# Which queue carries the empty instruction between two halves, and when a small transform may borrow a PSUM bank, in a combined convolution and feed-forward kernel

## The chip, the core and the metric

The kernel runs on one core of one Trainium2 chip. A core has a matrix engine (TensorE, PE in the profile), a vector engine (VectorE, DVE), an activation engine (ScalarE, ACT), a general engine (GpSimd, POOL) and a queue for transfers (SyncE, SP). Each engine takes the instructions of its own queue, and instructions on different engines are tied to each other by semaphores. Matmuls write to PSUM, a memory of banks from which VectorE and ScalarE read. The metric is the device time of one execution in microseconds; of the kernel before three executions are shown, and one more was recorded by the profiler.

## The reference

The input is a sequence of 2048 tokens of width 576. Two layers are run one after the other; each adds a long convolution block and a feed-forward block (FFN) to the stream:

```python
def _A_ref(q, k, v, shift_k, ssm_k, ssm_D):
    ...
    for t in range(ks):
        k_shift = k_shift + k_pad[:, t:t + S, :] * shift_k[:, ks - 1 - t][None, None, :]
    kv = k_shift * v
    ...
    y_f = kv_f * kf_f[None, :, :, :]
    y = (lambda x, s, axes=(-2,-1): jnp.fft.irfft2(x, s=s, axes=axes).astype(jnp.bfloat16))(y_f, (1, L), axes=(1, 2))[:, 0, :S, :]
    y = y + kv * ssm_D[None, None, :]
    return q * y

def _B_ref(x, w_gate, w_up, w_down):
    return (_gelu(x @ w_gate) * (x @ w_up)) @ w_down

x = A_q
x = x + _A_ref(_layernorm(x, axis=-1), A_k, A_v, A_shift_k, A_ssm_k, A_ssm_D)
x = x + _B_ref(_layernorm(x, axis=-1), B_w_gate, B_w_up, B_w_down)
x = x + _A_ref(_layernorm(x, axis=-1), A_k, A_v, A_shift_k, A_ssm_k, A_ssm_D)
x = x + _B_ref(_layernorm(x, axis=-1), B_w_gate, B_w_up, B_w_down)
```

The convolution's inner part (kv, its transform and the product with the transformed filter) is the same in both layers, since it doesn't depend on x. The inner width of the FFN is 4608.

## The kernel before

**Units and visits.** The tokens are cut into four chunks of 512, so that there are eight units (two layers by four chunks). The FFN of a unit is done in three phases of 1536 inner columns each, so that the weights of a phase can be shared between the units of a pass. There are five passes, with one, two, two, two and one units, and so 24 visits (here numbered from 1), each one unit by one phase. Visits 1 to 3 are the first unit's, 4 to 9 those of the next two units, 10 to 15 and 16 to 21 those of the passes after, and 22 to 24 the last unit's.

A visit has two stages. In the gate/up stage twelve tiles of 128 inner columns by 512 tokens are made, each by 18 matmuls that use 64 of PE's 128 rows at a time (L1081, tile gu). ScalarE applies the gelu and VectorE multiplies with the up half; the result, hT, stays in SBUF. There are two forms of this: in one (L1673, L1674) VectorE reads the up half out of PSUM and so is the one that frees the bank; in the other (L1664 to L1666) ScalarE copies the up half out too, and the bank is free before VectorE has come to it. The planner takes the second form where ScalarE is not booked far ahead (L1659 to L1674).

In the down stage (`two_rows`, called for rows 0 and 1 and then for rows 2 and 3) the four groups of 128 tokens are multiplied with the down weights, 192 half-row matmuls (L1735, tile dn) in all. A row group is accumulated in two steps: in step 0 the upper 64 rows of one operand half go to one bank and the lower 64 to the other, in step 1 the other way round. Between the two steps of the same bank pair stands `conv.hold`, an instruction that does nothing, on another engine's queue: it is made to name the bank pair, so that it waits for PE's step 0, and PE's step 1 waits for it. The transforms of the convolution (`both_steps`, `half_rows`; the matmul of `half_rows` is L310, tile cps) have the same two steps and the same instruction between them. In the trace it is an EVENT_SEMAPHORE of L1110. There are 150 of them: 54 of transforms and 96 of row groups.

When a row group is complete, VectorE adds it to the residual stream out of PSUM: L1771 in the first phase, L1773 or L1752 in the later ones, and L1765 in the last phase, where it also sums the row for the next layernorm.

**Layernorm statistics.** GpSimd computes the mean (`mean_after`, L911, tiles means and nm), ScalarE squares and sums (`square_task`, L919, tile junk), and GpSimd makes the reciprocal root from it (L926 tile ve, L927 tile rstd). The GpSimd instructions, with some DMAs, lie in a list (`conv.spills`) and are put into the program `AHEAD` = 2.0 us before the planner expects their input.

**Convolution among the visits.** The transforms, their products and the inverse of the convolution are cut into small pieces which the planner puts between tiles and row groups (`fill`). PE does the matmuls of a piece into a bank pair, ScalarE or VectorE takes the result out (eo L329, ab and cd L334, kc L633, and others). `fold` (L559, L560) is a group of eight additions and subtractions of VectorE, four for each of its two parts.

**PSUM.** There are four pairs of banks. Three of them rotate between the gate/up tiles and the row groups (`pr`, which sets `was[0]` to the time at which the planner expects the pair to be free). The fourth belongs to the convolution (`cps`). Where `conv.alt` is set, the next piece takes the next rotating pair in place of the fourth (`other`): here this is called borrowing. The pair after it then goes to a row group or a gate/up tile one place earlier in the rotation.

**What sets the order.** Nothing is moved by a compiler: the program is written in the order in which a planner, `Pace`, walks along. It keeps one clock each for PE, VectorE and ScalarE (`t.pe`, `t.dve`, `t.act`) and adds the constants C_... to them as it writes instructions. A piece is put in when its inputs are expected and its cost ends before a limit. `hurry()` is true until the planner has written the last row of the second chunk's convolution output. Each engine's queue is then in the order of writing. A changed clock anywhere can therefore change which piece comes next, on any engine.

Of the kernel before, what the change touches and what calls it, by code (L numbers as in the profile page):

```python
# [22 lines left out]
HW = 288  # L23
# [10 lines left out]
C_P0, C_P1, C_AC = 1.28, 1.35, 0.7  # L34
C_TT, C_ST, C_BN, C_NORM, C_HT, C_GELU, C_EVA, C_EVD, C_YH = 0.74, 0.80, 0.47, 0.62, 0.615, 0.51, 0.56, 0.72, 0.7
C_HB = 0.345
C_FOLD = 0.38
C_TURN, DRAIN = 0.0, 0.35
LAG = 0.25
AHEAD = 2.0  # L40
# [94 lines left out]
class Conv:  # L135
# [259 lines left out]
    def step(self, m, kv=None, loaded=False):  # L395
# [155 lines left out]
        def fold(sg):  # L551

            def run():
                if sg == 0:
                    w["free"] = self.acp.tile([P, 2, D], BF16, tag="ac", name="w")[:, 0, :]
                for plane in range(2):
                    a, b = z[plane, 0, sg][:], z[plane ^ sg, 1, sg][:]
                    up, down = (sg, sg + 2) if sg == 0 or plane else (sg + 2, sg)
                    nc.vector.tensor_tensor(out=w["free"], in0=a, in1=b, op=ALU.add)  # L559
                    nc.vector.tensor_tensor(out=a, in0=a, in1=b, op=ALU.subtract)  # L560
                    w[up, plane], w[down, plane], w["free"] = w["free"], a, b

                def fin(when):
                    for part in range(2):
                        mark(("z", sg, part), when + LAG)
                    if sg:
                        self.z_at[m] = when
                return fin
            return run
# [18 lines left out]
        for sg in range(2):  # L588
            self.V.append((now, 4 * C_FOLD, fold(sg)))
        ab = {}  # L590
# [175 lines left out]
def ssm_geglu_kernel(ctx, tc, A_q, A_k, A_v, A_shift_k, A_ssm_k, A_ssm_D, B_x, B_w_gate, B_w_up,  # L766
                     B_w_down, out):
    nc = tc.nc
# [21 lines left out]
    t = Pace()  # L790
# [10 lines left out]
    def bank(n, name, shape=(P, 2, 512), dt=F32):  # L801
        return banks[n].tile(list(shape), dt, tag="pr", name=name)
# [12 lines left out]
    def add_late():  # L815
        ready, n, run = late.popleft()
        run()
        bank_at[n % 3] = t.on_dve(C_EVD, ready) + 0.15

    bank_at, was = [0.0] * 3, [0.0]  # L820

    def pr(name):
        while late and taken[0] - late[0][1] >= 2:
            add_late()
        taken[0] += 1
        was[0] = bank_at[taken[0] % 3]
        bank_at[taken[0] % 3] = NEVER
        return bank(turn[(taken[0] - 1) % 3], name)
# [11 lines left out]
    conv = Conv(tc, ctx, t, gwork, xtp, A_k, A_v, A_shift_k, A_ssm_k, A_ssm_D, ident,  # L840
                lambda *form: bank(turn[3], "cps", *form), ypool)
# [265 lines left out]
        conv.ps_free[0] = xn_at[ui]  # L1107
        xn_done[ui] = j + 1

    conv.hold = lambda ps: nc.scalar.keepalive_nop([nc.scalar.lower_ap(ps[:, :, 0:HW])])  # L1110
    conv.slot = lambda: taken[0] % 3
    conv.borrowed = bank_at.__setitem__
    conv.alt_at = lambda: bank_at[(taken[0] + 1) % 3]
# [27 lines left out]
    def fill(limit, tensor, conv_first, between=None):  # L1141
        conv.run_open(t.pe)
        weights()
        conv.run_loads()
        spreads(tensor=tensor)
        while pressing() and run_aq(min(limit, t.pe + 2.3)):
            pass
        while True:
            if run_late(limit):
                continue  # L1150
            if conv_first:
                if not (conv.run_v(limit) or run_vq(limit)):
                    break
            elif not (run_vq(limit) or not pressing() and conv.run_v(limit)):
                break
        run_aq(min(limit, t.pe + 2.3))
        conv.between = between is not None
        if tensor and between is not None and not (1 in conv.z_at or conv.dry(between)):
            return
        if tensor:  # L1160
            for _ in range(3):
                if pressing() and (units[coming[0]][1], RT - 1) in conv.y_at or not conv.run_p():
                    break
# [16 lines left out]
    with tc.manual_schedule():  # L1180
# [6 lines left out]
        with ExitStack() as es:  # L1187
# [40 lines left out]
            ps = bank(3, "ps")  # L1228
# [379 lines left out]
        hurry = lambda: (1, RT - 1) not in conv.y_at  # L1608
# [4 lines left out]
        for at, (wb, ph, ui, first, final) in enumerate(visits):  # L1613
# [76 lines left out]
            def opened(j):  # L1690
                if j not in accs:
                    accs[j] = pr("dn"), taken[0]
                return accs[j]

            def row(j):

                acc, mine = opened(j)
                xh = x_c[c][:, j, :].rearrange("p (h d) -> p h d", h=2)

                def down(fi, h, acc):  # L1700
                    nc.tensor.matmul(acc[:, h, 0:HW], lhsT=hT[:, fi, j * P:(j + 1) * P],  # L1701
                                     rhs=wd[2 * wb + fi // WT][:, fi % WT, h * HW:(h + 1) * HW],
                                     start=(fi == 0), stop=(fi == FP - 1))
                if j == RT - 1:
                    dst = out2[c * CH:(c + 1) * CH, :].rearrange("(p j) d -> p j d", j=RT)[:, j, :]
                    for h in range(2):
                        if h:
                            acc = pr("dn")
                        for fi in range(FP):
                            down(fi, h, acc)  # L1710
                        ob, entry = out_tile()
                        entry[0] = True
                        nc.vector.tensor_tensor(out=ob[:, 0:HW], in0=xh[:, h, :], in1=acc[:, h, 0:HW], op=ALU.add)
                        nc.sync.dma_start(out=dst[:, h * HW:(h + 1) * HW], in_=ob[:, 0:HW])
                    return
                for fi in range(FP):
                    for h in range(2):
                        down(fi, h, acc)
                    t.pe += C_DN
                    if fi < FP - 1:  # L1720
                        fill(t.pe + 1.5, True, conv.left > 0)
                evict(j)

            def two_rows(j):

                order = ([(0, 0, fi) for fi in range(FP - 2)] + [(1, 0, fi) for fi in range(FP - 3)] +
                         [(0, 0, fi) for fi in range(FP - 2, FP)] + [(1, 0, fi) for fi in range(FP - 3, FP)] +
                         [(n, 1, fi) for n in range(2) for fi in range(FP)])
                for k, (n, step, fi) in enumerate(order):
                    acc, mine = opened(j + n)  # L1730
                    wn = wd[2 * wb + fi // WT][:, fi % WT, :]
                    lhs = hT[:, fi, (j + n) * P:(j + n + 1) * P]
                    for g in range(2):
                        r = slice((step ^ g) * HK, (step ^ g) * HK + HK)
                        nc.tensor.matmul(acc[:, g, 0:HW], lhsT=lhs[r], rhs=wn[r, g * HW:(g + 1) * HW],  # L1735
                                         start=step == 0 and fi == 0, stop=step == 1 and fi == FP - 1)
                    if step == 0 and fi == FP - 1:
                        conv.hold(acc)
                    t.pe += C_DN / 2
                    if step == 1 and fi == FP - 1:  # L1740
                        evict(j + n)
                    elif k % 2:
                        conv.alt = other
                        fill(t.pe + 1.5, True, conv.left > 0)

            def evict(j):
# [30 lines left out]

            conv.alt = other
            two_rows(0)
            if wb == NWB - 1:  # L1780
                conv.alt = None
                row(2)
                row(3)
            else:
                two_rows(2)
# [3 lines left out]
@with_exitstack  # L1789
def kernel(  # L1790
    ctx: ExitStack,
    tc: tile.TileContext,
    A_q: bass.AP,
    A_k: bass.AP,
    A_v: bass.AP,
    A_shift_k: bass.AP,
    A_ssm_k: bass.AP,
    A_ssm_D: bass.AP,
    B_x: bass.AP,
    B_w_gate: bass.AP,  # L1800
    B_w_up: bass.AP,
    B_w_down: bass.AP,
    out: bass.AP,
):
    ssm_geglu_kernel(tc, A_q, A_k, A_v, A_shift_k, A_ssm_k, A_ssm_D, B_x, B_w_gate, B_w_up,
                     B_w_down, out)
# [30 lines left out]
```

## Time and profile before

| what | us |
|---|---|
| median of the three runs | 913.64 |
| lowest and highest of them | 913.34 to 914.93 |
| profiled execution, whole | 913.37 |
| its span in the trace | 911.5 |
| one visit without gaps: gate/up stage, down stage | 23.31 + 11.76 |

A row of the timeline reads: start in us, duration in us, engine, line, operation, tile written and tiles read, shape, xN for N instructions drawn together, and in brackets how long the engine had been idle before it and which instruction's end released it. Where PE is concerned the ends are modelled, so the length of a gap is taken here from the starts of the groups and from the time that one more matmul in a group takes. An engine name with a q behind it (ACTq, POOLq) is that engine's sequencer, which runs the semaphore events. The span is split at the start of the first visit, 40.2 us after the span's start, ahead of which the first layernorm, the load of the inputs and the first convolution work lie; the last visit's work ends near 908.

### The profile page before, as it was taken

To read this page: it belongs to the slowest core of one execution; us is meant where nothing else is said; L and a number is where in the kernel's file an instruction comes from. 1 tells how busy PE (TensorE), PEld (TensorE's weight loads), DVE (VectorE), ACT (ScalarE), POOL (GpSimd) and SP (SyncE) were. 2 spreads that over 40 slices of the span, in tenths; PEclk is the share of its full clock that TensorE was granted. 3 is DMA by queue.
4 is the path that set the end of the run, shared out by engine and by line. 5 is a ranking of instruction groups with operands and counts; after the bars stand their busy time and mean duration, and the time that the engine had idled before them with its cause. 6 is when DMAs were issued, how large, how long until landed. Compare 5 with 4: busy or idle time off the path is not lost.

```text
span 911.5 us, 24246 instructions
## 1 busy us (share of the span) xinstructions
PE 904.0 (99%) x10451; PEld 600.2 (66%) x10451; DVE 565.1 (62%) x1129; ACT 363.2 (40%) x675; POOL 146.8 (16%) x311
## 2 busy tenths in 40 slices
PE   9999999999999999999999999999999999999998
PEld 7757656466576675765766757757757657667666
DVE  8888985885789886677888843553332334433332
ACT  7785445735425356354244223451121224321211
POOL 5533003220113012230023001220000002100000
PEclk9999999999999999999999999999999999999999
DMA  9999977449619604974934702772720820777630
GB/s 247 307 250 275 249 164 144 113 126 235 201 53 231 142 2 79 271 186 106 247 121 117 167 16 58 129 137 60 142 79 2 157 79 13 143 176 180 136 101 27
DMA packets 125839, 129.12 MB, mean 142 GB/s; under 512 B 40866, under 2 KB 118051, under 8 KB 125732
## 3 DMA queue, kind: packets, MB, share of 16 engines
q1 hardware_dynamic: 116706, 92.63, 47.8%
q0 software_dynamic: 8880, 34.36, 11.4%
q8 instruction: 81, 1.33, 0.6%
q10 hardware_dynamic: 146, 0.59, 0.2%
q14 instruction: 26, 0.21, 0.1%
HBM read 106.91 MB, written 11.80 MB: 130 GB/s over the span
## 4 chain that ended last, share of the span: by engine, by line
PE 94%; DVE 4%; ACT 1%; issue 1%; POOL 0%; ACTq 0%
PE gu L1081 58%; PE dn L1735 29%; PE cps L310 2%; PE ps L284 2%; DVE kvt L255 1%; PE dn L1701 1%; DVE kvt L261 1%; DVE kc L633 0%; PE ps L1317 0%; DVE hT L1666 0%; DVE cd L334 0%; PE ps L1452 0%; PE ps L1081 0%; DVE hh L633 0%; POOL rstd L1537 0%
## 5 line engine op out<-in xcount | busy, mean ns | idle before, releaser
L1081 PE MATMUL gu<-xnT,wgu 64*128 64x512 bf16 x5148 | 561.0, 376 | 1.1 <-DVE hT L1674 0.9
L1081 PEld LDWEIGHTS <-wgu 64*128 64x128 bf16 x5220 | 293.5, 94 | 262.3 <-issue 2.3
L1735 PE MATMUL dn<-wd,hT 64*128 64x288 bf16 x4512 | 294.6, 283 | 0.8 <-ACTq L1110 0.4
L1735 PEld LDWEIGHTS <-hT 64*128 64x128 bf16 x4512 | 253.3, 94 | 28.7 <-issue 1.6
L1673 ACT ACTIVATE ga<-gu 128x512 f32<-128x512 f32 x175 | 104.4, 597 | 318.9 <-PE gu L1081 312.7
L1674 DVE TENSOR_TENSOR hT<-ga,gu 128x512 bf16<-128x512 f32 x175 | 120.0, 686 | 172.5 <-ACT ga L1673 172.0
L1664 ACT ACTIVATE ga<-gu 128x512 bf16<-128x512 f32 x111 | 66.2, 597 | 148.4 <-PE gu L1081 140.6
L1666 DVE TENSOR_TENSOR hT<-ga 128x512 bf16<-128x512 bf16 x112 | 46.9, 421 | 54.7 <-ACT ga L1665 54.7
L1665 ACT CAST ga<-gu 128x512 bf16<-128x512 f32 x111 | 64.4, 580 | 0.0
L911 POOL TENSOR_SCALAR means<-s 128x1 f32<-128x1 f32 x28 | 16.9, 606 | 245.1 <-DVE x_c L1765 216.8
L1773 DVE TENSOR_TENSOR x_c<-x_c,dn 128x576 f32<-128x576 f32 x32 | 23.9, 751 | 26.3 <-PE dn L1735 26.2
L1771 DVE SCALAR_TENSOR_TENSOR x_c<-dn,means,x_c 128x576 f32<-128x576 f32 x28 | 22.8, 815 | 24.5 <-PE dn L1735 24.4
L927 POOL TENSOR_TENSOR rstd<-ve,neghalf_t 128x1 f32<-128x1 f32 x56 | 34.9, 623 | 4.7
L329 ACT ACTIVATE eo<-cps 128x576 f32<-128x576 f32 x40 | 25.6, 657 | 21.3 <-PE cps L310 16.7
L346 DVE TENSOR_TENSOR prod<-prod 128x576 bf16<-128x576 bf16 x64 | 29.3, 458 | 2.2
L1752 DVE TENSOR_TENSOR xn<-x_c,dn 128x576 bf16<-128x576 f32 x15 | 11.3, 753 | 26.0 <-PE dn L1735 23.6
L633 DVE TENSOR_TENSOR kc<-ab,cd 128x288 bf16<-128x288 f32 x64 | 25.5, 451 | 0.0
L444 POOL DMA_DIRECT2D kr<-Kd x20 | 11.0, 552 | 85.9 <-DVE prod L345 85.9
L911 POOL TENSOR_SCALAR nm<-s 128x1 f32<-128x1 f32 x28 | 7.9, 281 | 94.8 <-DVE x_c L965 94.7
L919 ACT ACTIVATE junk<-x_c,nm 128x576 bf16<-128x576 f32 x28 | 21.5, 767 | 4.0 <-POOL nm L911 3.5
L955 ACT ACTIVATE yh<-y,rstd 128x576 f32<-128x576 bf16 x28 | 21.2, 768 | 2.3 <-PE dn L1735 1.4
L449 POOL DMA_DIRECT2D hr<-Hd x32 | 17.6, 551 | 21.4 <-DVE prod L345 19.9
(180 smaller groups left out, 629.9 us busy)
## 6 DMA issues: line engine op xcount, KB each, us to landing
wgu<-in_B_w_gate_dram SPq DMA_DIRECT2D x45, 576.0 KB, 6.0
wd<-in_B_w_down_dram SPq DMA_DIRECT2D x30, 864.0 KB, 6.5
wgu<-in_B_w_up_dram SPq DMA_DIRECT2D x45, 512.0 KB, 9.0
hr<-Hd POOLq DMA_DIRECT2D x32, 288.0 KB, 4.7
kr<-Kd POOLq DMA_DIRECT2D x24, 288.0 KB, 4.5
Kd<-kc POOLq DMA_DIRECT2D x12, 288.0 KB, 5.1
k<-in_A_k_dram POOLq DMA_DIRECT2D x3, 1008.0 KB, 10.9
wgu<-in_B_w_up_dram SPq DMA_DIRECT2D x45, 64.0 KB, 7.9
```

Of the source, the lines that this page charges most:

```text
L329: nc.scalar.activation(out=eo[:], in_=ps[:, :, 0:HW], func=ACT.Copy, scale=scale)
L346: nc.vector.tensor_tensor(out=dst[:, cols], in0=pr[:, 0, cols], in1=pr[:, 1, cols], op=ALU.subtract if part == 0 else ALU.add)
L633: nc.vector.tensor_tensor(out=into[k][:, plane, cols], in0=a, in1=b, op=op)
L911: nc.gpsimd.tensor_scalar(out=v["nm"][:], in0=v["s"][:], scalar1=-1.0 / D, scalar2=None, op0=ALU.mult)
L927: nc.gpsimd.tensor_tensor(out=v["rstd"][:], in0=ve[:], in1=neghalf_t[:, 0:1], op=ALU.pow)
L1081: nc.tensor.matmul(cols(pair[:, s, :]), lhsT=w[r0:r0 + HK, k, gi * P:(gi + 1) * P], rhs=cols(xnT[r0:r0 + HK, blk_of[k], :]), start=(k == 0 ...
L1664: nc.scalar.activation(out=ga[:, 0, :], in_=pair[:, 0, :], func=ACT.Gelu_apprx_tanh)
L1665: nc.scalar.copy(out=ga[:, 1, :], in_=pair[:, 1, :])
L1666: nc.vector.tensor_tensor(out=hT[:, fi, :], in0=ga[:, 0, :], in1=ga[:, 1, :], op=ALU.mult)
L1673: nc.scalar.activation(out=ga[:], in_=pair[:, 0, :], func=ACT.Gelu_apprx_tanh)
L1674: nc.vector.tensor_tensor(out=hT[:, fi, :], in0=ga[:], in1=pair[:, 1, :], op=ALU.mult)
L1735: nc.tensor.matmul(acc[:, g, 0:HW], lhsT=lhs[r], rhs=wn[r, g * HW:(g + 1) * HW], start=step == 0 and fi == 0, stop=step == 1 and fi == FP - 1)
```

## The change

Four edits. The empty instruction goes to ScalarE's queue only where the planner's clock for ScalarE is not over 0.1 us ahead of that of PE, and to GpSimd's queue otherwise. In the down stage a transform may borrow a rotating pair only in the second pair of rows, or where `hurry()` is true; before, it might in both. When a row group is opened, PE's clock is set to the time at which its bank pair is expected to be free, if that is later; before, only gate/up tiles did this. The cost that the planner books for one of the fold's operations is 0.46 and not 0.38.

```diff
-C_FOLD = 0.38
+C_FOLD = 0.46
...
-    conv.hold = lambda ps: nc.scalar.keepalive_nop([nc.scalar.lower_ap(ps[:, :, 0:HW])])
+    def hold(ps):
+
+        eng = nc.scalar if t.act <= t.pe + 0.1 else nc.gpsimd
+        eng.keepalive_nop([eng.lower_ap(ps[:, :, 0:HW])])
+    conv.hold = hold
...
             def opened(j):
                 if j not in accs:
                     accs[j] = pr("dn"), taken[0]
+                    t.pe = max(t.pe, was[0])
                 return accs[j]
...
                     elif k % 2:
-                        conv.alt = other
+                        conv.alt = other if hurry() or j == 2 else None
                         fill(t.pe + 1.5, True, conv.left > 0)
```

The changed program has as many instructions on PE as before (20904 rows of its queue), and 93 of the empty instructions on ScalarE's queue and 57 on GpSimd's.

## The prediction

> **What bounds the kernel now.** I read the page's engine table and its chain of waits first, then the list of what the matmul engine waited for, then the timeline around each of those waits.
>
> ```profile
> span 911.5 us, 24246 instructions
> PE 904.0 (99%) x10451; PEld 600.2 (66%) x10451; DVE 565.1 (62%) x1129; ACT 363.2 (40%) x675; POOL 146.8 (16%) x311
> PEclk9999999999999999999999999999999999999999
> PE 94%; DVE 4%; ACT 1%; issue 1%; POOL 0%; ACTq 0%
> ```
>
> PE is busy for 904.0 of 911.5 us, it is 94% of the chain that ended last, and its clock is never cut. The change leaves PE's work as it is, so only the gaps in PE's order can shrink or grow.
>
> ```profile
> PE gu L1081 <- DVE hT L1674: 0.9, 1, 0.9
> PE dn L1735 <- ACTq L1110: 0.4, 1, 0.4
> PE cps L310 <- ACTq L1110: 0.4, 1, 0.4
> PE dn L1735 <- DVE x_c L1771: 0.3, 2, 0.2
> ```
>
> (columns: total us, times, longest). These four, behind a start-up wait and a wait at the end that the change does not touch, are all that the profile calls waits of PE after its loops begin. Two are the empty instruction (L1110) on ScalarE's queue, one is the fold, two times it is a row's eviction: the change aims at each. What one of them really costs is read from the next rows, since a matmul row's end is modelled.
>
> ```profile
> 65.69 0.42 PE L1735 MATMUL dn<-wd,hT 64*128 64x288 bf16 x4
> 66.49 0.30 PE L310 MATMUL cps<-ht,T 64*128 64x288 bf16 x2 [0.38 <-ACTq L1110]
> 338.72 1.89 PE L1735 MATMUL dn<-wd,hT 64*128 64x288 bf16 x28
> 183.77 0.53 PE L1735 MATMUL dn<-wd,hT 64*128 64x288 bf16 x6
> 184.71 1.40 PE L1735 MATMUL dn<-wd,hT 64*128 64x288 bf16 x20 [0.42 <-ACTq L1110]
> ```
>
> A group of 28 takes 1.89 and one of 6 takes 0.53, so a further half-row matmul is (1.89-0.53)/22 = 0.062 us (0.061 over longer groups). Four from 65.69 should end by 65.94; the next started at 66.49: 0.55 lost in visit 1. In the same way 183.77 + 6 x 0.061 = 184.14 against 184.71: 0.57 in visit 4.
>
> **Part 1, the empty instruction on GpSimd.** All 150 are on ScalarE now. In the changed program 57 of them go to GpSimd, by count of its queue; the rest stay. The rule sends one there when the planner has ScalarE booked past PE, and ScalarE is then often at the statistics pass (L919, junk) whose result GpSimd's own next instruction (L926, ve) waits for. What is ahead of the empty instruction on GpSimd is therefore what decides.
>
> In visit 1's down stage the changed GpSimd order is ve, rstd for row groups 2 and 3, then two empty instructions (those that wait at 66.4 now), then ve for group 4.
>
> ```profile
> L1110 ACTq EVENT_SEMAPHORE  x2: 17/17/17, 66.4 to 66.5; - x2
> 68.10 0.19 POOL L926 TENSOR_SCALAR ve<-ss 128x1 f32<-128x1 f32 x1 [0.91 <-ACT junk L919]
> 68.37 0.55 POOL L927 TENSOR_TENSOR rstd<-ve,neghalf_t 128x1 f32<-128x1 f32 x1
> 69.93 0.27 POOL L926 TENSOR_SCALAR ve<-ss 128x1 f32<-128x1 f32 x1 [1.01 <-ACT junk L919]
> 68.60 0.30 PE L310 MATMUL cps<-ht,T 64*128 64x288 bf16 x2
> ```
>
> The ve ahead of them starts at 68.10, when ScalarE's junk is there (its bracket says so); ScalarE's order up to there does not hang on PE. Does a waiting ve hold up the empty instruction behind it? No instruction of this kind stands on GpSimd behind a wait at present except the semaphore event of one load:
>
> ```profile
> 178.22 0.42 POOL L926 TENSOR_SCALAR ve<-ss 128x1 f32<-128x1 f32 x1 [1.05 <-ACT junk L919]
> L237 POOLq EVENT_SEMAPHORE  x1: 43/43/43, 178.7 to 178.7; - x1
> 178.72 0.55 POOL L927 TENSOR_TENSOR rstd<-ve,neghalf_t 128x1 f32<-128x1 f32 x1
> ```
>
> It stands between ve and rstd, and ran at 178.7, after ve had waited and ended, just ahead of rstd. I take it that the queue is in order and that the empty instruction runs about when the last rstd ahead of it starts: 68.33 in visit 1. With the 0.07 that lie now between the event (66.4) and the matmul (66.49), PE goes on at 68.40 and not at 66.49: +1.9. PE's later slack in that stage absorbs 0.28 (68.60 is 0.16 late now, and 70.44 0.12), and a third empty instruction behind the ve of 69.93 gives back about 0.15. **Visit 1: +1.8** (+1.4 to +2.1: the lower end if it need not wait for ve's end, only for its start, and another wait goes with it).
>
> The event rows and the Trainium skill can be set side by side here. The Trainium skill ("Perfetto Trace Analysis", section "GPSIMD Engine Instruction") says that an instruction is pushed into a hardware wait queue, after which the sequencer is free for the next one, before the semaphores are satisfied; by that an instruction of the sequencer alone could overtake a waiting ve. The trace's event at 178.7 speaks against it; by the rule this sum would lose 3.2 us, and rival A is what comes out.
>
> Visit 3 has the same pattern: ve, rstd, two empty instructions of the first row pair, then two more ve.
>
> ```profile
> L1110 ACTq EVENT_SEMAPHORE  x2: 17/17/17, 146.2 to 146.6; - x2
> 147.50 0.19 POOL L926 TENSOR_SCALAR ve<-ss 128x1 f32<-128x1 f32 x1 [0.68 <-ACT junk L919]
> 147.78 0.57 POOL L927 TENSOR_TENSOR rstd<-ve,neghalf_t 128x1 f32<-128x1 f32 x1
> ```
>
> Now the two events run at 146.2 and 146.6, and PE needs the first at about 146.4 without waiting. Behind this ve it comes at 147.74, and PE at 147.80. **Visit 3: +1.4** (+1.1 to +1.6).
>
> Visit 4 loses its 0.57, since GpSimd's queue is empty there, but VectorE is without a pause:
>
> ```profile
> 180.00:196.00 16.00, 15.58 (x239) 12.83 (x237) 15.22 (x33) 4.77 (x8) 0.61 (x1) 1.00 0.52 131
> 193.36 0.81 DVE L1771 SCALAR_TENSOR_TENSOR x_c<-dn,means,x_c 128x576 f32<-128x576 f32 x1
> 194.26 6.01 PE L1081 MATMUL gu<-xnT,wgu 64*128 64x512 bf16 x54
> 340.64 0.61 PE L1081 MATMUL gu<-xnT,wgu 64*128 64x512 bf16 x4
> ```
>
> (busy us by engine in the order PE, weight loads, VectorE, ScalarE, GpSimd: VectorE 15.22 of 16.) The first gate/up tile of the next visit takes the bank that row 2's eviction (193.36 to 194.17) frees, and starts at 194.26, right behind it. PE that comes 0.57 earlier waits there for 0.5: **-0.05** (-0.57 to 0). In visit 8 empty instructions stand behind ve, means and nm; the same working gives 0.38 lost; now it loses 0.21 (338.72 + 28 x 0.061 = 340.43 against 340.64) and some 0.15 in two smaller slips, 0.36: **0** (-0.4 to +0.6). The other GpSimd ones have an idle queue or come after rstd has begun: 0, hidden behind PE's own matmuls between two steps.
>
> **Part 2, the borrowed bank.** Now a transform may borrow the next rotating bank in both row pairs; then only in the second, or when the planner hurries. Visits 5 and 10 are alike:
>
> ```profile
> 225.17 1.16 PE L1735 MATMUL dn<-wd,hT 64*128 64x288 bf16 x16
> 226.50 0.67 PE L1735 MATMUL dn<-wd,hT 64*128 64x288 bf16 x8 [0.17 <-DVE x_c L1771]
> 230.39 0.82 DVE L1771 SCALAR_TENSOR_TENSOR x_c<-dn,means,x_c 128x576 f32<-128x576 f32 x1
> 231.13 0.81 DVE L633 TENSOR_TENSOR kc<-ab,cd 128x288 bf16<-128x288 f32 x2
> 231.64 5.58 PE L1081 MATMUL gu<-xnT,wgu 64*128 64x512 bf16 x50
> 407.78 0.67 PE L1735 MATMUL dn<-wd,hT 64*128 64x288 bf16 x8
> 408.63 0.67 PE L1735 MATMUL dn<-wd,hT 64*128 64x288 bf16 x8 [0.17 <-DVE x_c L1771]
> 365.79 8.45 PE L1735 MATMUL dn<-wd,hT 64*128 64x288 bf16 x132
> ```
>
> 225.17 + 16 x 0.061 = 226.15 against 226.50, and 407.78 + 8 x 0.061 = 408.27 against 408.63: 0.35 each, gone if row 2 no longer takes a bank whose eviction is late. What is late next: with a borrow in the second pair, the next gate/up tile waits for row 2's eviction, which ends at 231.21; PE, now 0.35 earlier, comes at 231.29, with some 0.08 to spare. I take **-0.30 each** (-0.35 to +0.2, one more VectorE pair of 0.73 ahead of the eviction giving the upper end). Visit 9: 132 matmuls at 0.061 and the 0.18 by which a group's last one is drawn longer are 8.26, the row has 8.45: **-0.19** (-0.19 to 0).
>
> **Part 3, the fold's cost and the row's opening time.** These move VectorE's work among the gate/up tiles.
>
> ```profile
> 521.78 5.14 PE L1081 MATMUL gu<-xnT,wgu 64*128 64x512 bf16 x46
> 523.32 0.45 DVE L559 TENSOR_TENSOR w<-yb 128x576 bf16<-128x576 bf16 x1
> 523.81 0.46 DVE L560 TENSOR_TENSOR yb<-yb 128x576 bf16<-128x576 bf16 x1
> 527.87 0.82 PE L1081 MATMUL gu<-xnT,wgu 64*128 64x512 bf16 x6 [0.94 <-DVE hT L1674]
> ```
>
> The eight operations go at 0.49 each (523.32, 523.81), 3.9 in all to 527.2, one after the other; hT, which frees the bank, comes behind them. 46 matmuls at 0.108 (12 tiles of 18 in 23.31) should have ended at 526.75: 1.12 lost. In the changed order four of the eight come, then an hT of the form that frees its bank from ScalarE (L1664 to L1666), then the other four; the bank is free some 0.45 before PE needs it. **Visit 14: -1.12** (-1.12 to -0.9).
>
> **The sum**: 1.8 + 1.4 - 0.05 + 0 - 0.60 - 0.19 - 1.12 = +1.24. Against the profiled execution (913.37, of which 911.5 are span) that is 914.6. The median of the runs shown (913.64) is 0.27 above it: **914.9**, 0.14% above. All lower ends together give -0.8 (1.4 + 1.1 - 0.57 - 0.4 - 0.7 - 0.19 - 1.12 = -0.5, less 0.3 for other moves of VectorE's order), all upper ends +4.2 (2.1 + 1.6 + 0.6 + 0.4 - 0.9 = 3.8 and 0.4): 912.8 to 917.8, the outer microsecond unlikely on either side.
>
> **Rival A: GpSimd's queue does not hold the empty instruction up, and the change does what it says.** For it: events on the sequencer are 17 to 43 ns each, and GpSimd is idle five sixths of the span. Against it: the event at 178.7. Visit 1 is then -0.55, visit 3 0, visit 8 -0.36, with the other terms as above: -0.55 - 0.05 - 0.36 - 0.60 - 0.19 - 1.12 = -2.9, so 910.8; with visit 4's 0.57 whole, 910.3. Say 910.5. Chance 0.17.
>
> **Rival B: slower, because the second pair's borrow puts the next visit's first tile behind row 2's eviction.** The place is the join of down and gate/up stage in visits 5, 8 and 10; it decides as soon as one more pair of VectorE operations (0.73 apart, as 230.39 to 231.13) is ahead of L1771. For it: 0.08 to spare, and VectorE at 15.22 of 16 in the like stage of visit 4. Against it: PE's delays ahead of it give VectorE time. Each join then costs 0.65 more than in the sum in visits 5 and 10, and 0.5 in visit 8: +1.8, on top of 1.24, so 916.7. Chance 0.28.
>
> **How the numbers follow.** The forecast has 0.55, A 0.17, B 0.28. Within 0.2% is within 1.83 us, about what can be told here: 911.8 to 915.5. A gives faster, but for its upper edge: 0.15, and 0.02 from the forecast's lower end: 0.17. B gives 0.26 slower; the forecast's upper third, where visits 1 and 3 cost more, 0.11: 0.37. Same is what is left, 0.46. The range runs from 911.0, which leaves out most of A, to 917.0, which leaves out the upper half of B's spread.
>
> **What would show it.** Right: in visit 1 a wait of PE's cps (L310) on GpSimd's queue of about 1.9 that ends with ve and rstd, in visit 3 one of dn (L1735) of 1.4, and no wait for hT (L1674) in visit 14. Wrong: an empty instruction that runs on GpSimd while a ve ahead of it still waits (A), or gate/up tiles that wait for L1771 at the joins (B). Waits at other GpSimd instructions, the DMA issues among them, would make the count of delayed ones wrong.

## The result and the profile after

The changed kernel takes 915.27 us in the median of 20 runs (914.70 to 917.51), the kernel before 913.43 us in 20 runs beside them (913.07 to 914.93). The ratio is 1.0023, with a 95% interval of 1.0016 to 1.0029: slower by 0.2%. The span in the trace went from 911.5 to 912.9.

PE's work (10451 matmuls) and its clock are as before, so the page's first lines hardly differ. The list of what PE waited for does (line, what it waited for: total us, times, longest). These are its lines for the visits' matmuls in the changed kernel; one of 0.2 in visit 1, where the kernel before loses as much, is left out:

```profile
PE cps L310 <- POOLq L1113: 2.3, 1, 2.3
PE dn L1740 <- POOLq L1113: 1.2, 1, 1.2
...
PE gu L1081 <- DVE x_c L1776: 0.4, 1, 0.4
```

The wait for hT (0.9), both for the empty instruction on ScalarE (0.4 each) and the two for a row's eviction (L1771, 0.3 together) are gone. In their place stand two on GpSimd's queue (L1113 is the empty instruction's line now, L1740 that of the down matmuls) and another one for a row's eviction, at a gate/up tile. The timeline of visit 1's down stage of the changed kernel, GpSimd, PE and the events of L1113 between 67.5 and 69 us:

```profile
67.89 0.19 POOL L926 TENSOR_SCALAR ve<-ss 128x1 f32<-128x1 f32 x1 [0.91 <-ACT junk L919]
68.17 0.55 POOL L927 TENSOR_TENSOR rstd<-ve,neghalf_t 128x1 f32<-128x1 f32 x1
L1113 POOLq EVENT_SEMAPHORE  x2: 17/17/17, 68.1 to 68.2; - x2
65.50 0.42 PE L1740 MATMUL dn<-wd,hT 64*128 64x288 bf16 x4
68.20 0.30 PE L310 MATMUL cps<-ht,T 64*128 64x288 bf16 x2 [2.28 <-POOLq L1113]
```

In the program's order the two empty instructions stand behind this ve and this rstd, and rstd itself waits for ve's result. The first runs at 68.1, when ve has ended (67.89 + 0.19 = 68.08), the second at 68.2, while rstd has 0.5 still to run, and PE goes on at 68.20. Its work had been done at 65.50 + 4 x 0.061 = 65.74: 2.46 lost in one place. Visit 3 of the changed kernel, the same views:

```profile
149.41 0.19 POOL L926 TENSOR_SCALAR ve<-ss 128x1 f32<-128x1 f32 x1 [0.68 <-ACT junk L919]
149.69 0.57 POOL L927 TENSOR_TENSOR rstd<-ve,neghalf_t 128x1 f32<-128x1 f32 x1
L1113 POOLq EVENT_SEMAPHORE  x2: 17/17/17, 149.6 to 149.7; - x2
147.83 0.65 PE L1740 MATMUL dn<-wd,hT 64*128 64x288 bf16 x8
149.71 1.52 PE L1740 MATMUL dn<-wd,hT 64*128 64x288 bf16 x22 [1.23 <-POOLq L1113]
```

147.83 + 8 x 0.061 = 148.32 against 149.71: 1.39.

To see all visits at once I take each stage's length, from its first matmul to the next stage's first, and take off its matmuls (0.061 for a half-row matmul of 288 columns, 0.108 for one of 512). What is left is what PE lost there. The stages in which something changes, in us, for the two kernels and the experiments below:

| stage | before | after | hold_only | all_but_hold | ve_later | visits_1_3_on_scalar | guarded | guarded_v4 |
|---|---|---|---|---|---|---|---|---|
| start-up | 6.16 | 5.94 | 5.93 | 5.93 | 6.08 | 5.99 | 5.94 | 5.94 |
| 1, down | 1.15 | 3.28 | 3.28 | 1.16 | 1.46 | 1.15 | 1.18 | 1.16 |
| 3, down | 0.47 | 1.88 | 1.88 | 0.47 | 0.72 | 0.47 | 0.47 | 0.47 |
| 4, gate/up | 0 | 0 | 0 | 0 | 0 | 0 | 0 | 0.16 |
| 4, down | 0.58 | 0.55 | 0.55 | 0.55 | 0.55 | 0.55 | 0.55 | 0.15 |
| 5, down | 0.34 | 0.19 | 1.78 | 0.18 | 0.18 | 0.18 | 0.19 | 0.19 |
| 8, down | 0.37 | 0.17 | 1.30 | 0 | 0.02 | 0.17 | 0 | 0 |
| 9, down | 0.19 | 0 | 0.20 | 0 | 0 | 0 | 0 | 0 |
| 10, down | 0.35 | 0.18 | 0.35 | 0.19 | 0.17 | 0.17 | 0.19 | 0.19 |
| 14, gate/up | 1.12 | 0 | 1.12 | 0 | 0 | 0 | 0 | 0 |

From the first visit on, the changed kernel loses 2.13 + 1.41 - 0.03 - 0.15 - 0.20 - 0.19 - 0.17 - 1.12 = 1.68 us more. The start-up, which the change does not touch, was 0.2 longer in the profile of before than in that of the changed kernel (0.1 to 0.2 longer than in all the others), so the spans differ by 1.4 only. The lowest of 20 runs against the lowest of 20 (914.70 and 913.07) differ by 1.63, close to the table's 1.68. The medians differ by 1.84, because nine of the changed kernel's 20 runs lie some 1.5 us above the other eleven, and no profile of one of the nine is there to show why.

### The profile page after: what moved, and what is told of

It reads as the page before. It is cut to its first block, busy times and chain, and to the rows that moved or that the text cites. A ratio compares the mean times of both kernels' runs of the same rounds, so it can differ in the third digit from the quotient of the medians.

```text
span 912.9 us, 24250 instructions
## 1 busy us (share of the span) xinstructions
PE 903.5 (99%) x10451; PEld 599.9 (66%) x10451; DVE 563.4 (62%) x1128; ACT 365.3 (40%) x678; POOL 145.9 (16%) x311
## 4 chain that ended last, share of the span: by engine, by line
PE 94%; DVE 3%; ACT 1%; POOL 1%; issue 0%; POOLq 0%; ACTq 0%
PE gu L1081 59%; PE dn L1740 29%; PE cps L310 2%; PE ps L284 2%; DVE kvt L255 1%; PE dn L1706 1%; DVE kvt L261 0%; PE ps L1321 0%; PE ps L1456 0%; PE ps L1081 0%; DVE hT L1670 0%; DVE hh L633 0%; DVE ab L334 0%; POOL rstd L1541 0%; PE ps L1234 0%
## 5 line engine op out<-in xcount | busy, mean ns | idle before, releaser
L1740 PE MATMUL dn<-wd,hT 64*128 64x288 bf16 x4512 | 294.4, 283 | 1.4 <-POOLq L1113 1.2
L1740 PEld LDWEIGHTS <-hT 64*128 64x128 bf16 x4512 | 253.3, 94 | 28.9 <-issue 1.8
L1668 ACT ACTIVATE ga<-gu 128x512 bf16<-128x512 f32 x113 | 67.5, 597 | 146.5 <-PE gu L1081 138.0
L911 POOL TENSOR_SCALAR means<-s 128x1 f32<-128x1 f32 x28 | 16.0, 573 | 241.2 <-DVE x_c L1770 214.8
L1776 DVE SCALAR_TENSOR_TENSOR x_c<-dn,means,x_c 128x576 f32<-128x576 f32 x28 | 22.8, 815 | 26.2 <-PE dn L1740 26.2
L329 ACT ACTIVATE eo<-cps 128x576 f32<-128x576 f32 x40 | 26.0, 653 | 27.0 <-PE cps L310 19.6
L911 POOL TENSOR_SCALAR nm<-s 128x1 f32<-128x1 f32 x28 | 8.0, 287 | 96.5 <-DVE x_c L965 96.5
```

The lines of the kernel that those rows point to most:

```text
L329: nc.scalar.activation(out=eo[:], in_=ps[:, :, 0:HW], func=ACT.Copy, scale=scale)
L1668: nc.scalar.activation(out=ga[:, 0, :], in_=pair[:, 0, :], func=ACT.Gelu_apprx_tanh)
```

## The experiments

The theory: an empty instruction on GpSimd waits in an in-order queue for everything ahead of it, a waiting ve above all. Rival 1: the empty instruction is slow on GpSimd wherever it stands. Rival 2: the other edits' new order makes the waits. All diffs are against the kernel named and show what is changed; the runs write `hold` and `opened` on one line each, so that line numbers in rows of the experiments are those of the kernel before.

| kernel | median, us | ratio to before, 95% interval | span |
|---|---|---|---|
| hold_only | 919.92 | 1.0076 (1.0061 to 1.0091) | 917.1 |
| all_but_hold | 911.26 | 0.9975 (0.9966 to 0.9985) | 909.2 |
| ve_later | 911.73 | 0.9985 (0.9976 to 0.9994) | 909.9 |
| visits_1_3_on_scalar | 911.41 | 0.9982 (0.9972 to 0.9991) | 909.4 |
| fold_only | 912.01 | 0.9988 (0.9977 to 0.9998) | 910.2 |
| borrow_only | 911.94 | 0.9987 (0.9976 to 0.9997) | 910.0 |
| opening_only | 912.73 | 0.9997 (0.9987 to 1.0007) | 910.8 |
| guarded | 911.37 | 0.9982 (0.9973 to 0.9992) | 909.3 |
| guarded_v4 | 910.91 | 0.9974 (0.9965 to 0.9984) | 909.0 |

**The empty instruction alone**, against the kernel before:

```diff
-    conv.hold = lambda ps: nc.scalar.keepalive_nop([nc.scalar.lower_ap(ps[:, :, 0:HW])])
+    conv.hold = lambda ps: (lambda eng: eng.keepalive_nop([eng.lower_ap(ps[:, :, 0:HW])]))(
+        nc.scalar if t.act <= t.pe + 0.1 else nc.gpsimd)
```

> The kernel before with one edit: the empty instruction goes to GpSimd where the planner has ScalarE booked past PE; 62 of 150 move. Theory (GpSimd's queue is in order, and an empty instruction waits there behind a ve that waits for junk): PE waits 2.4 us in visit 1 and 1.4 us in visit 3 as in the changed kernel, visit 4 loses its 0.57 wait and gets one of 0.5 at the next gate/up tile, visit 14 keeps its 1.1 us wait for hT. The span is 3.0 to 3.6 us longer than before, the time 916.5 to 917.2. Rival 1 (the empty instruction is slow on GpSimd wherever it stands): many small waits at GpSimd's events, some tenths each, beside the two. Rival 2 (the other edits' new order makes the waits): the span within 0.5 us of before.

Visits 1 and 3 are as in the changed kernel to 0.01 us, so this edit alone makes their waits, and rival 2 falls. But the time is 2.7 us over the upper end expected (median of four runs; the profiled one, 919.13, is 1.9 over): visits 5 and 8 lose 1.4 and 0.9 more, which the expectation had at nothing. In visit 5 no ve stands ahead; GpSimd's rows of this kernel around PE's stop, with the event and PE:

```profile
232.27 0.54 POOL L444 DMA_DIRECT2D kr<-Kd  x1 [26.43 <-PE dn L1735]
...
233.86 1.06 POOL L449 DMA_DIRECT2D hr<-Hd  x2
234.92 0.54 POOL L444 DMA_DIRECT2D kr<-Kd  x1
L1110 POOLq EVENT_SEMAPHORE  x1: 17/17/17, 234.8 to 234.8; - x1
231.74 1.90 PE L1735 MATMUL dn<-wd,hT 64*128 64x288 bf16 x28
234.89 1.38 PE L1735 MATMUL dn<-wd,hT 64*128 64x288 bf16 x19 [1.25 <-POOLq L1110]
```

In the queue's order seven DMA issues stand ahead of the empty instruction, 0.53 each from 232.27 on. Its event came at 234.8, when the fifth was ending and two were still to run; PE's step was done at 231.74 + 28 x 0.061 = 233.46 and waited 1.43. So DMA issues hold the queue too, though not to the end of the last one. With the other three edits the order is another one, and this place doesn't come up in the changed kernel.

**All but the empty instruction**, against the changed kernel: all 150 on ScalarE.

```diff
-        eng = nc.scalar if t.act <= t.pe + 0.1 else nc.gpsimd
+        eng = nc.scalar
```

> The changed kernel with all 150 empty instructions on ScalarE as before; the three other edits stay. Theory: the waits of visits 1 and 3 on GpSimd are gone, visit 1 has its old 0.55 and visit 4 its old 0.57 on ScalarE's queue; what the other edits save stays: 1.1 in visit 14, 0.2 in visit 9, 0.15 to 0.2 each in visits 5 and 10. Span 909.7 to 910.1, time 911.5 to 912.0, 0.2% under before. Rival 2 (the other edits make the waits): over 912.5 in span.

Measured 911.26, below the range and faster than both kernels; the span of 909.2 is 0.5 under its range, since the start-up is 0.2 shorter than in the profile of before and visit 8's 0.37 is gone, neither of which was expected. Visits 1 and 3 are back at 1.16 and 0.47. The move to GpSimd costs the changed kernel 2.12 + 1.41 + 0.17 = 3.7 us, which is the difference of the spans (912.9 - 909.2). Visit 4 loses 0.55 with either engine, but in other places: here 0.40 at an empty instruction of ScalarE and some 0.15 at the next gate/up tile.

**ve and rstd later in GpSimd's queue**, against the changed kernel. Number and engine of the empty instructions stay:

```diff
-            conv.spills.append((when - AHEAD, root))
+            conv.spills.append((when - 0.3, root))
```

> The changed kernel with the same 57 empty instructions on GpSimd, but ve and rstd are put into GpSimd's queue 0.3 us before junk is expected to be done and not 2.0 us before, so that in visits 1 and 3 they stand behind the empty instructions. Theory: the waits of 2.4 and 1.4 us vanish, visit 1 loses about 0.6 us to ScalarE's tiles as before, and all that the changed kernel saves stays: span 909.0 to 909.8, time 910.8 to 911.6. Rival 1 (the empty instruction is slow on GpSimd): the span stays at 912.9 within 0.5 us, since their number and engine are the same.

This is the run that tells the theory from rival 1. PE's waits on GpSimd in visits 1 and 3 fall from 2.46 and 1.39 to 0.73 and 0.24, the span to 909.9 (0.1 over the range). The rest is again the queue. In visit 3 the empty instructions stand ahead of ve now, but behind three nm (L911), and the first runs at 146.8, just before the last nm starts; near the end of visit 1 another 0.28 is lost behind DMA issues (L378), as in the changed kernel. The place of the long wait in visit 1 of this kernel:

```profile
66.31 0.19 POOL L926 TENSOR_SCALAR ve<-ss 128x1 f32<-128x1 f32 x1 [1.58 <-ACT junk L919]
66.58 0.55 POOL L927 TENSOR_TENSOR rstd<-ve,neghalf_t 128x1 f32<-128x1 f32 x1
L1110 POOLq EVENT_SEMAPHORE  x2: 17/17/17, 66.5 to 66.6; - x2
66.61 0.30 PE L310 MATMUL cps<-ht,T 64*128 64x288 bf16 x2 [0.55 <-POOLq L1110]
```

The empty instructions now stand behind the ve of the row group before (66.31) and run when its rstd starts. Moving two other instructions in the queue moved the wait by 1.7 us, from one rstd to the one before it.

**The empty instructions of visits 1 and 3 back on ScalarE**, 19 of the 57, against the changed kernel:

```diff
-        eng = nc.scalar if t.act <= t.pe + 0.1 else nc.gpsimd
+        eng = nc.scalar if t.act <= t.pe + 0.1 or at in (0, 2) else nc.gpsimd
```

> The changed kernel with the 19 empty instructions of visits 1 and 3 back on ScalarE; the other 38 stay on GpSimd. Theory (only those that stand behind a waiting instruction cost): visit 1 loses 1.15 as before and visit 3 0.47, so 2.1 + 1.4 - 1.1 = 2.4 us less than the changed kernel, and with the wait at the next gate/up tile of visit 4 in place of the old one: span 909.3 to 909.7 with the start-up as in before, time 911.2 to 911.6. Rival 1 (each of them costs about the same): a third of what hold costs comes back, 1.1 us, so span 911.5 to 912.0.

Span 909.4 and 911.41 in the median: these 19 carry 3.5 of the 3.7 us. Of the 38 that stay on GpSimd only one makes PE wait, 0.17 in visit 8. Rival 1's span of 911.5 to 912.0 is out: the other 37 are on GpSimd as well and cost nothing that shows.

**One edit each of the other three**, against the kernel before (each is one of the lines of the change's diff).

> The kernel before with one edit: the fold's cost is 0.46. Theory: the eight fold operations are split in two with an hT between them, whose bank ScalarE frees; visit 14's wait of 1.12 us is gone and nothing else changes on PE: span 910.2 to 910.6. Rival (another edit splits the fold): visit 14 keeps 1.12.

> The kernel before with one edit: a transform borrows a rotating pair in the second pair of rows only, or where hurry() holds. Theory: the waits for a row's eviction in visits 5 and 10 (0.35 each) turn into the smaller ones for eo that the changed kernel has (0.15 to 0.2), visit 8 and 9 lose 0.2 less each, visit 14 keeps its 1.12: span 0.5 to 0.9 under before, 910.6 to 911.0.

> The kernel before with one edit: PE's planned clock is moved to the opening time of a row group's bank. Theory: it only reorders VectorE and ScalarE where PE does not wait; PE's losses by visit stay as before within 0.2 us each, span 911.2 to 911.8.

fold_only: visit 14 loses nothing, the other visits are within 0.04 of before. borrow_only: visits 5 and 10 at 0.19 each and visit 9 at 0, as expected; visit 8 went from 0.37 to 0 where 0.2 less was expected, and visit 14 to 0.73 where no change was. opening_only: visit 14 loses nothing there too, and visits 4, 5 and 10 lose 0.2 more each, to ScalarE's empty instruction. So fold_only's span is at the lower end of its range, and borrow_only's 910.0 and opening_only's 910.8 are under theirs, by 0.6 and 0.4. VectorE's rows of the two kernels in visit 14, first fold_only, then opening_only:

```profile
524.66 0.46 DVE L560 TENSOR_TENSOR yb<-yb 128x576 bf16<-128x576 bf16 x1
525.03 0.42 DVE L1666 TENSOR_TENSOR hT<-ga 128x512 bf16<-128x512 bf16 x1
525.37 0.45 DVE L559 TENSOR_TENSOR yb<-yb 128x576 bf16<-128x576 bf16 x1
```

```profile
524.52 0.46 DVE L560 TENSOR_TENSOR yb<-yb 128x576 bf16<-128x576 bf16 x1
524.89 0.68 DVE L1674 TENSOR_TENSOR hT<-ga,gu 128x512 bf16<-128x512 f32 x1
```

In both, an hT follows the fourth fold operation and not the eighth. So the fold's cost is enough to split the group, but not the only edit that does: the opening time does it too, at 0.7 lost in other places. Each edit that moves the planner's clocks can change this order; the borrow's alone left 0.73 of the wait.

**A guard**, against the changed kernel: in both runs the planner keeps a clock of GpSimd's queue, and in guarded_v4 alone visit 4's second pair of rows borrows nothing (the last pair of lines).

```diff
+    pool_at = [0.0]
...
-            self.spills.popleft()[1]()
+            self.pool_at[0] = max(self.pool_at[0], self.t.pe) + 0.55; self.spills.popleft()[1]()
...
+            conv.pool_at[0] = max(conv.pool_at[0], t.pe, when)
...
+                conv.pool_at[0] = max(conv.pool_at[0], t.pe, when) + 0.4
...
-        eng = nc.scalar if t.act <= t.pe + 0.1 else nc.gpsimd
+        eng = nc.scalar if t.act <= t.pe + 0.1 or conv.pool_at[0] > t.pe + 0.1 else nc.gpsimd
...
-                        conv.alt = other if hurry() or j == 2 else None
+                        conv.alt = other if (hurry() or j == 2) and (at != 3 or j == 0) else None
```

> The changed kernel with two additions: the empty instruction goes to GpSimd only where no ve, rstd, mean or DMA issue is planned there past PE's clock (39 of 150), and in visit 4 no transform borrows in the second pair of rows. Theory: visits 1 and 3 lose 1.15 and 0.47 as before; visit 4's 0.55, which moved from ScalarE's queue to row 2's eviction, is gone too, as the first gate/up tile of visit 5 gets another pair; the rest as in the changed kernel: span 908.5 to 908.9, time 910.4 to 910.9. Rival (visit 4's wait moves on to the transforms or a third place): 0.3 to 0.6 us lost there again, span 909.0 to 909.4.

> The changed kernel with the first of the two additions alone: the empty instruction goes to GpSimd only where nothing is planned there past PE's clock. It splits what guarded_v4 did. Theory: visits 1 and 3 as in before (1.16 and 0.47 lost), visit 4 loses its 0.55 at the next visit's first gate/up tile, behind row 2's eviction (L1771), and no wait for a transposed DMA or for eo stands in visit 4; span 909.2 to 909.5, so that visit 4's edit was worth 0.2 to 0.5. Rival (the guard by itself moves the small waits at 157 and 191): they are here too, and visit 4's edit was worth the whole 0.55.

The guard alone gives a span of 909.3, with no wait on GpSimd's queue longer than 0.1 us, and visit 4 loses its 0.55 at the next gate/up tile. Without the borrow that wait is gone, but smaller ones come. The join of visits 4 and 5 in the guarded kernel, then visit 4 and the join in guarded_v4:

```profile
194.06 5.14 PE L1081 MATMUL gu<-xnT,wgu 64*128 64x512 bf16 x46 [0.39 <-DVE x_c L1771]
```

```profile
190.33 1.02 PE L1735 MATMUL dn<-wd,hT 64*128 64x288 bf16 x14
191.34 0.30 PE L310 MATMUL cps<-ht,T 64*128 64x288 bf16 x2
...
192.07 1.89 PE L1735 MATMUL dn<-wd,hT 64*128 64x288 bf16 x28
193.79 1.48 PE L1081 MATMUL gu<-xnT,wgu 64*128 64x512 bf16 x12
```

192.07 + 28 x 0.061 = 193.79: the first gate/up tile no longer waits. 190.33 + 14 x 0.061 = 191.19 against 191.34: 0.15 lost instead, to a transform that no longer borrows. Another 0.16 stands in visit 4's gate/up stage; it is a wait for a transposed transfer ahead of the place of the edit, and one execution doesn't tell whether the edit has to do with it. By visit 4's down stage the edit was worth 0.40, with that wait 0.24 (0.3 by the spans): some of the wait moved on, as the rival had it, but not all. Its span of 909.0 lies at the lower end of the rival's range, 0.1 over the theory's. guarded_v4's 0.9974 and all_but_hold's 0.9975 can't be told apart; both are faster than both kernels, and all_but_hold is the simpler one.

## Why the prediction was right

The forecast was 914.9, with 0.46 for no difference beyond 0.2% and 0.37 for slower; measured 915.27 and a ratio of 1.0023, just past the edge between the two, so that the outcome given 0.37 came. The terms of the sum against the stages:

| term | predicted | measured |
|---|---|---|
| visit 1 | +1.8 | +2.13 |
| visit 3 | +1.4 | +1.41 |
| visit 4 | -0.05 | -0.03 |
| visit 8 | 0 | -0.20 |
| visits 5 and 10 | -0.60 | -0.32 |
| visit 9 | -0.19 | -0.19 |
| visit 14 | -1.12 | -1.12 |
| sum | +1.24 | +1.68 |

The two large terms and the mechanism behind them were right. That the sum is only 0.44 off is in part luck, since visit 8's error of -0.20 makes up for some of the +0.33 of visit 1 and the +0.28 of visits 5 and 10.

*Visits 1 and 3.* The step that carried the forecast, that the empty instruction runs when the last rstd ahead of it starts, held to some hundredths: the wait of visit 1 is 0.55 + 1.91 = 2.46. Its one piece of evidence was misread, though to no harm: in the program's order the event of L237 doesn't stand between ve and rstd but behind rstd, where the empty instructions of visits 1 and 3 stand too. It also waits for two transfers, so that it couldn't have settled the question alone. all_but_hold shows that the engine is the cause, ve_later that it is the order in GpSimd's queue. The absorbed 0.28 and the third empty instruction's 0.15 (0.17 measured) came as said. What was mis-sized is the rest of visit 1: "the other GpSimd ones have an idle queue" was put at 0 for all of them, and one does not. GpSimd and PE of the changed kernel near the end of visit 1:

```profile
78.94 2.15 POOL L378 DMA_DIRECT2D Hd<-hh  x4 [5.64 <-DVE kc L334]
L1113 POOLq EVENT_SEMAPHORE  x2: 17/17/17, 78.4 to 80.4; - x2
80.01 0.30 PE L310 MATMUL cps<-v,nT 64*128 64x288 bf16 x2
80.44 0.67 PE L1740 MATMUL dn<-wd,hT 64*128 64x288 bf16 x8
```

It stands behind the four DMA issues of GpSimd and runs at 80.4, when the third is under way and the fourth has yet to start (80.55); PE loses 80.44 - (80.01 + 2 x 0.061) = 0.31. The prediction's last part had named them as what would make the count wrong; its sum left them out.

*Visit 4.* The wait went from ScalarE's queue to the eviction, as worked out. The changed kernel's rows, VectorE and PE:

```profile
196.69 0.81 DVE L1776 SCALAR_TENSOR_TENSOR x_c<-dn,means,x_c 128x576 f32<-128x576 f32 x1
195.78 1.39 PE L1740 MATMUL dn<-wd,hT 64*128 64x288 bf16 x20
197.56 1.69 PE L1081 MATMUL gu<-xnT,wgu 64*128 64x512 bf16 x14 [0.39 <-DVE x_c L1776]
```

PE was through at 195.78 + 20 x 0.061 = 197.00 and got the bank when L1776 had ended, at 197.50. guarded_v4 confirms it from the other side: without the borrow in that pair the wait at the tile is gone.

*Visits 5 and 10.* The eviction's wait went (borrow_only: 0.19 left), but half the gain was given back to another wait than the one looked for:

```profile
232.14 1.90 PE L1740 MATMUL dn<-wd,hT 64*128 64x288 bf16 x28
234.01 0.30 PE L310 MATMUL cps<-v,T 64*128 64x288 bf16 x2
```

232.14 + 28 x 0.061 = 233.85 against 234.01: 0.16. A transform that no longer borrows takes the convolution's own pair, and waits until ScalarE has taken the last one out of it (eo, L329, by the semaphore that this matmul waits for). The prediction asked only what is late next among the rotating pairs.

*Visits 8 and 14.* Visit 8 was estimated at 0.38 lost and lost 0.17: of its empty instructions only one came late, and the 0.37 of before went to 0 by the borrowing rule (borrow_only), so the term came to -0.20 and not 0. Visit 14's size was exact and the split of the fold is what made it. Part 3 put it down to the fold's cost and the opening time together; each of them does it alone, and which of them acts in the changed kernel isn't told apart.

*The rivals.* A (the queue does not hold the empty instruction up) fell with the first row of visit 1. The rule of the Trainium skill weighed there ("Perfetto Trace Analysis", section "GPSIMD Engine Instruction"), by which the sequencer is free for the next instruction before the semaphores of the one ahead are satisfied, does not describe what GpSimd's queue did here: the events of visits 1 and 3 ran at 68.1 and 149.6, after the ve ahead of them had waited and run, when the rstd that waits for it was let go. B (the next visit's first tile behind row 2's eviction) didn't occur in visits 5, 8 and 10; only visit 4 has it, where the sum had it.

## What to carry to other kernels

An instruction that does nothing showed no price of its own here; its price was what stood ahead of it in its queue. Before moving it to an engine that is idle on average, look at what that engine's queue is waiting for at that moment. If the rule for moving it is "the other engine is busy", and this engine waits for just that engine's result, the move puts it behind the very wait that it was to avoid.

A small gain in one place is found again as a wait at the next resource in half of the places here (visits 4, 5 and 10, but not 8, 9 and 14): price a removed stall by what is late next, over all the pairs and queues that the freed work now uses.

## What the runs showed of the hardware

The event of an empty instruction takes 17 ns on GpSimd as on ScalarE, and of the 38 on GpSimd outside visits 1 and 3 of the changed kernel 37 cost PE nothing. In visits 1 and 3 an event behind a ve that waited for ScalarE and an rstd that waited for ve ran between ve's end and rstd's start (68.08 and 68.17 in visit 1), and the second event ran while rstd still had 0.5 us to go: they waited until the instruction ahead of them was let go, not until it had ended. DMA issues of GpSimd, 0.53 us each, hold an event behind them too (1.43 us of PE in visit 5 of hold_only), but let it go when the last two of seven had yet to run, and in visit 1 of the changed kernel the last one of four.
